# Weight pieces, filler matmuls and store ranks in a planned attention-and-experts kernel

## The chip, the cores and the metric

The kernel runs on one core of a Trainium2 chip. The metric is the device time of one execution in microseconds (us). Six runs of the kernel before gave a median of 307.6 us (307.2 to 310.36). The engines of the core are named as in the profile: PE (TensorE, matmuls; PEld is its weight loading), DVE (VectorE), ACT (ScalarE), POOL (GpSimd) and SP (SyncE, which here only issues transfers).

## What is computed

A gated linear attention with 4 batches, 8 heads, 768 steps and 48 values per head feeds a mixture of 4 experts over 3072 tokens of 384 values, all in float32.

```python
f = 1.0 / (1.0 + np.exp(-f_logit))
for t in range(S):
    state = f[:, :, t, :, None] * state + np.einsum('bhd,bhe->bhde', k[:, :, t], v[:, :, t])
    y[:, :, t] = np.einsum('bhd,bhde->bhe', q[:, :, t], state)
x = y.transpose(0, 2, 1, 3).reshape(B * S, H * D)
p = domain_probs / (domain_probs.sum(-1, keepdims=True) + 1e-09)
for e in range(4):
    out += p[:, e:e + 1] * (np.maximum(x @ w1[e], 0.0) @ w2[e])
```

Here w1[e] is 384 x 1024 and w2[e] is 1024 x 384.

## The kernel before

The 768 steps are cut into six chunks (c = 0 to 5) of 128. For each chunk and batch, attention is done in blocks: the gate (L256, L260), its running sum by a matmul (L264), exponentials (L274, L276), scaled q and k (L288), their transposes (by PE, L297, in chunks 0 and 1, by DMA, L301, later), scores (L312) and their mask (L316), the result y (L323, L327), its transpose into xT (L352 or L305), and the state carried to the next chunk (L333, L340, L347, L348). The last row of the exponentials goes through a small transfer named egs (L283).

A chunk then has 512 tokens (4 batches of 128) for the experts. For each expert e and each block fc of 128 of the 1024 hidden columns, three matmuls over the 384 inputs make h (L356), and ReLU on ACT or DVE (L364, L362) writes it as bf16. For each batch nt, eight matmuls over the hidden blocks, in two halves of four, make the output (L368); it is scaled by p and added to an output tile "o" (L377 or L379 for expert 0, L375 for the others). After expert 3 the tile is stored (L383). In chunk 0, and in chunk 1 for some experts, h is made in two halves of 256 tokens, because the second two batches' attention is done later.

Weights come by POOL's DMA queue in nine pieces (L398 to L409): expert 0's w1 in two halves of columns, then w1 of 1, w2 of 0, w1 of 2, w2 of 1, w1 of 3, w2 of 2, w2 of 3. The first is issued when the last q of chunk 0 has landed. The load of chunk 1's f, batch 1 (L230), waits for the third piece from the end; the last piece waits for k of chunk 1. All other loads, stores, egs and DMA transposes are issued by SP, in one order.

The order of everything is written at build time by a small planner (class Plan, L26 to L99). Each step has a cost on the engines that may do it, a number for its rank (prio, lower goes first), dependencies, and buffers ("rooms") that it takes and frees. Whenever a planned engine is free, the planner gives it the lowest number among the steps that are ready (L73 to L89). DMA is one such engine. A step is ready (L40) when each step before it has ended, plus a latency and that step's lag. The steps are then emitted in the planned order, and the hardware's engines each work through their own list in that order, waiting by semaphores. So a planned time only sets the order.

Rooms: four PSUM banks for h and output sums (ps_m), four for attention (ps_t), six output tiles "o" (four are filled in one chunk), four each for f, q, k, v. Ranks in the expert part go by a running unit (L546 to L552): a step of h has the unit's number, output matmuls that plus 0.5. Chunk 0 has units 0 to 39, its last expert's outputs are units 40 to 47, and chunk 2's loads have 30 to 37 (L577 to L580).

Before the first h, PE's planned gaps are filled with matmuls on a tile of ones (L584 to L595), one for each 0.2 us of gap.

Of the kernel before, what the change touches and what calls it, by code (L numbers as in the profile page):

```python
# [9 lines left out]
BF16 = mybir.dt.bfloat16  # L10
# [15 lines left out]
class Plan:  # L26
# [13 lines left out]
    def ready(self, o, e):  # L40

        t = 0.0
        for d in o.deps:
            if d.end is None:
                return None
            t = max(t, d.end + d.lag + (self.LATENCY if d.engine != e else 0.05))
        return t

    def take(self, o):
# [53 lines left out]
def kernel(  # L103
# [11 lines left out]
    nc = tc.nc  # L115
    B, H, S, D = q.shape
# [7 lines left out]
    E, Din, F = moe_w1.shape  # L124
    KD = Din // 128
    KF = F // 128
    NT = B * T
# [6 lines left out]
    wk = ctx.enter_context(tc.tile_pool(name="wk", bufs=1))  # L134
# [4 lines left out]
    P = Plan(rooms)  # L139


    busy = wk.tile([128, 256], BF16, name="busy")
    nc.vector.memset(busy, 1.0)  # L143
    nc.scalar.preload_act_table_set("natural_log_exp_and_others")
    U = const.tile([T, T], FP32)
# [8 lines left out]
    for nm, nb in (("gp", 2), ("qk", 2)):  # L154
        for i in range(rooms[nm]):
            t = pads[nm, i] = const.tile([T, nb, H, P2], BF16, name=f"{nm}{i}")
# [4 lines left out]
        out=mask01, in_=mask01, compare_op=ALU.is_ge, fill=0.0,  # L161
# [5 lines left out]
    for i in range(2):  # L167
        t = const.tile([MP, B, NP, 2 * D], BF16, name=f"sb{i}")
# [16 lines left out]
    ins = {}  # L185
# [10 lines left out]
    def tl(kind, *key):  # L196

        if (kind, key) not in tiles:
            room = kind if kind in rooms else "ps_m" if kind in ("hp", "op", "pp") else "ps_t"
            slot = P.slot[(room, kind) + key if room.startswith("ps_") else (room,) + key]  # L200
            if room in ("gp", "qk"):
                tiles[kind, key] = pads[room, slot]
            else:
                shape, dt = shapes[kind]
                pool = ps if room.startswith("ps_") else wk
                tiles[kind, key] = pool.tile(shape, dt, name=f"{room}{slot}")
        return tiles[kind, key]

    def after(later, earlier):
        tc.add_manual_dep(later.ins, earlier.ins.name,  # L210
                          mybir.DependencyInfo(mybir.DependencyClass.Sync, mybir.DependencyReason.DATA),
                          reason="order of transfers")
# [17 lines left out]
        if (c, nm, b) == (1, "f", 1):  # L230
            after(ins[c, nm, b], ins["w", w_gate])

    def load_w(i, e, which, cols):
        w, r = (w1_sb, w1_r) if which == 1 else (w2_sb, w2_r)
        ins["w", i] = nc.gpsimd.dma_start(out=w[:, e, :, cols], in_=r[e][:, :, cols])  # L235
        if i == w_gate + 2:
            after(ins["w", i], ins[1, "k", 0])
        if i == 0:
            after(ins["w", 0], ins[0, "q", B - 1])


    def load_p():
# [138 lines left out]
    def store(c, nt, cols):  # L381
        r0 = nt * S + c * T
        nc.sync.dma_start(out=out[r0:r0 + T, cols], in_=tl("o", c, nt)[:, cols])  # L383


    ld = {}
    def add_load(c, nm, b, n, prio, deps=(), cost=None):
        op = P.add(f"ld {nm}{c}.{b}", {"DMA": cost or 1.05 * n}, lambda e: load(c, nm, b, n), prio,
                   deps=deps, takes=[(nm, c, b // 2)], lag=2.0)
        for i in range(n):  # L390
            ld[c, nm, b + i] = op
        return op

    for i, x in enumerate("f0 k0 q0 f1 k1 q1 f2 f3 k2 q2 v0 k3 q3 v1 v2 v3".split()):
        add_load(0, x[0], int(x[1]), 1, -1000 + i)
    add_load(1, "f", 0, 1, -980, cost=0.1)

    pieces = [(0, 1, slice(0, F // 2)), (0, 1, slice(F // 2, F))] + [  # L398
        (e, which, slice(0, F if which == 1 else Din)) for e, which in ((1, 1), (0, 2), (2, 1), (1, 2), (3, 1), (2, 2), (3, 2))]
    wd, w_gate = {}, len(pieces) - 3  # L400
    for i, (e, which, cols) in enumerate(pieces):
        if i == w_gate + 2:
            for x in ((1, "f", 1, 1), (1, "k", 0, 2), (1, "q", 0, 2), (1, "v", 0, 2)):
                add_load(*x, -430 + len(ld), deps=wd[3, 1])
        iss = P.add(f"w issue {i}", {"POOL": 0.8}, lambda _, i=i, x=(e, which, cols): load_w(i, *x),
                    -500 + i, deps=[ld[0, "q", B - 1]] + ([ld[1, "k", 0]] if i > w_gate + 1 else []))
        op = P.add(f"w {i}", {"DMA": 2.25 if i < 2 else 4.5}, lambda _: None,
                   -500 + (0, 0.5, 1, 2, 3, 4, 5, 6, 111)[i], deps=[iss], lag=1.5)
        wd[e, which] = wd.get((e, which), []) + [op]  # L409
    for x in ((1, "f", 2, 2), (1, "k", 2, 2), (1, "q", 2, 2), (1, "v", 2, 2)):  # L410
        add_load(*x, -400 + len(ld), deps=wd[3, 1])
# [2 lines left out]
    xdone, kvdone = {}, {}  # L414
# [94 lines left out]
    hdone, omm, oev = {}, {}, {}  # L509

    def add_h(c, e, fc, n0, n1, xs):
        p, n = unit[0], n1 - n0
        key = ("ps_m", "hp", c, e, fc, n0)
        m = P.add(f"h {c}.{e}.{fc}.{n0}", {"PE": 0.645 * n / NT}, lambda _: mm_h(c, e, fc, n0, n1), p,
                  deps=(wd[e, 1] if (c, e) != (0, 0) else [wd[0, 1][fc * 2 // KF]]) + [t for b in xs for t in xdone[c, b]], takes=[key], lag=0.2, frees=[("xT", c)])
        hdone[c, e, fc, n0] = P.add(f"relu {c}.{e}.{fc}.{n0}",
                                    {"ACT": 0.6, "DVE": 0.69} if n == NT else {"ACT": 0.39, "DVE": 0.42},
                                    lambda g: relu(c, e, fc, n0, n1, g), p - 3, deps=[m],
                                    takes=[("h", c, e)], frees=[key])

    def add_o(c, e, nt, half):
        p = unit[0] + 0.5
        by_cols = (c, e, nt) == (C - 1, E - 1, B - 1)
        part = half if by_cols else 0
        cols = slice(half * Din // 2, (half + 1) * Din // 2) if by_cols else slice(0, Din)
        fcs = range(KF) if by_cols else range(half * 4, half * 4 + 4)
        key = ("ps_m", "op", c, e, nt, part)
        d = [hdone[k] for k in hdone if k[:2] == (c, e) and k[2] in fcs and k[3] <= nt * T]
        m = omm[c, e, nt] = P.add(f"o {c}.{e}.{nt}.{half}", {"PE": 0.645}, lambda _: mm_o(c, e, nt, fcs, part, cols), p,
                                  deps=d + wd[e, 2] + [omm.get((c, e, nt))], takes=[key], lag=0.2, frees=[("h", c, e)])  # L530
        if half == 1 or by_cols:
            w = 0.36 if by_cols else 0.62
            ev = oev[c, e, nt] = P.add(f"ev_o {c}.{e}.{nt}.{part}", {"ACT": 0.58, "DVE": 0.56} if e == 0 else {"DVE": w},
                                       lambda g: ev_o(c, e, nt, part, cols, g), p - 1,
                                       deps=[m, oev.get((c, e - 1, nt)), pdone], takes=[("o", c, nt)], frees=[key])
            if e == E - 1:
                P.add(f"store {c}.{nt}.{part}", {"DMA": 0.6}, lambda _: store(c, nt, cols), p, deps=[ev], frees=[("o", c, nt)])

    attention(0, lambda b, s: -200 + 3.6 * b + s * 0.8, 1)
    pl = P.add("ld p", {"ACT": 0.1}, lambda e: load_p(), -1100, lag=3.0)  # L540
# [2 lines left out]
    ALL, LO, HI = list(range(B)), [0, 1], [2, 3]  # L543
    N2 = NT // 2

    def zip_units(hs, os):  # L546
        for i in range(max(len(hs), len(os))):
            if i < len(hs):
                add_h(*hs[i])
            if i < len(os):  # L550
                add_o(*os[i])
            unit[0] += 1  # L552

    def hl(c, e, n0, n1, xs):
        return [(c, e, fc, n0, n1, xs) for fc in range(KF)]
# [4 lines left out]
    for c in range(C):  # L560
        u0 = unit[0]
        if c == 0:
            for n0, n1, xs in ((0, N2, LO), (N2, NT, HI)):
                zip_units(hl(c, 0, n0, n1, xs), [])
        elif c == 1:
            zip_units([], ol(0, E - 1, ALL))
            for n0, n1, xs in ((0, N2, LO), (N2, NT, HI)):
                zip_units(hl(c, 0, n0, n1, xs), [])
                zip_units(hl(c, 1, n0, n1, xs), ol(c, 0, xs))
        else:  # L570
            zip_units(hl(c, 0, 0, NT, ALL), ol(c - 1, E - 1, ALL))
        for e in range(2 if c == 1 else 1, E):
            zip_units(hl(c, e, 0, NT, ALL), ol(c, e - 1, ALL))
        if c + 1 < C:
            base = u0 + (0 if c else 10)
            attention(c + 1, lambda b, s, base=base: base + 2 + 5 * b + s, 2)
        if c + 2 < C:  # L577
            for half in range(2):
                for j, nm in enumerate("fkqv"):
                    add_load(c + 2, nm, 2 * half, 2, u0 + 30 + 4 * half + j, deps=wd[3, 1])  # L580
# [5 lines left out]
    spare = ps.tile([128, 512], FP32, name="ps_m3")  # L586
    t = 2.5
    for o in done:
        if o.engine == "PE" and o.start <= first:
            o.pad, t = int((o.start - t) / 0.2), o.end  # L590
    if PRINT:
        PRINT(done)
    for o in done:
        for _ in range(o.pad):
            nc.tensor.matmul(out=spare[:, 0:256], lhsT=busy[:, 0:128], rhs=busy, start=True, stop=True)  # L595
        o.emit(o.engine)


# [31 lines left out]
```

## Time and profile before

| what | us |
|---|---|
| median of six runs | 307.6 |
| the profiled execution | 307.2 |
| its span, first to last instruction | 305.4 |
| PE busy | 291.9 |
| ACT, DVE, POOL busy | 171.9, 131.9, 96.4 |
| first h matmul | 23.05 |
| last matmul ends | about 302 |

The profile is of one execution. A page gives totals by engine, 40 slices of the span, and the costliest groups of instructions; the trace behind it answers for waits (who stood idle, and what ended it), for the chain of work that ended last, for a timeline, and for busy time in stretches. In a timeline line the first two numbers are the start and the duration in us, and the bracket is the idle time of that engine before it and what released it; "x4" merges four instructions. A line number is one of the kernel before. PEclk is the clock that was granted to PE. On SP, a line's duration is the time in which the issue held the queue, not the transfer.

### The profile page before, as it was taken

The page shows a single profiled execution, that of the slowest core. Times are in us where ns is not written, and L with a number is a line of the kernel's source. Part 1 is how long each engine was busy: PE and PEld are TensorE (multiplying, and loading weights), DVE is VectorE, ACT ScalarE, POOL GpSimd, SP SyncE. Part 2 cuts the span into 40 slices and gives each one's busy share as a digit, 9 for nine tenths or more (in the row PEclk, how much of TensorE's full clock was granted, in tenths as well). Part 3 has the DMA queues.
Part 4 walks back from the last instruction along what each step waited for, and adds up shares of the span by engine and source line. Part 5 has one row for each costly group of instructions (what it writes and reads, how often), then busy time and mean ns, then how long its engine had stood idle before and what let it go on. Part 6 is the DMA issues. An engine that isn't in the chain of part 4 may idle for free.

```text
span 305.4 us, 5535 instructions
## 1 busy us (share of the span) xinstructions
PE 291.9 (96%) x2121; PEld 171.1 (56%) x2151; DVE 131.9 (43%) x251; ACT 171.9 (56%) x308; POOL 96.4 (32%) x159
## 2 busy tenths in 40 slices
PE   7869999999997999999999999999999999999995
PEld 5648555557774566455555555565555555555553
DVE  5676003588852376506373335363325252201223
ACT  4765763766766464677454676444566444465440
POOL 4384501325676045442624442622232100000000
PEclk9997999999999999999999999999999999999999
DMA  8999999990997539969799988200422300100003
GB/s 150 202 168 207 207 208 200 187 136 2 186 204 164 109 77 179 195 159 169 114 211 165 219 171 150 49 15 13 114 60 50 49 15 24 70 22 2 0 0 105
DMA packets 134639, 36.10 MB, mean 118 GB/s; under 512 B 125372, under 2 KB 133436, under 8 KB 134612
## 3 DMA queue, kind: packets, MB, share of 16 engines
q1 hardware_dynamic: 128416, 29.40, 53.9%
q0 software_dynamic: 6160, 6.29, 12.6%
q8 instruction: 17, 0.28, 0.4%
q14 instruction: 10, 0.08, 0.1%
q10 hardware_dynamic: 36, 0.05, 0.1%
HBM read 31.51 MB, written 4.72 MB: 119 GB/s over the span
## 4 chain that ended last, share of the span: by engine, by line
PE 86%; DMA 7%; SPq 4%; issue 1%; DVE 1%; ACT 0%
PE ps_m L368 40%; PE ps_m L356 39%; SPq L228 3%; DMA w_sb<-in_moe_w_dram 2%; PE ps_t L312 2%; DMA out_dram<-o 2%; DMA q<-in_q_dram 2%; PE ps_t L327 1%; PE ps_t L333 1%; PE ps_t L323 1%; DMA QK<-qk 1%; PE ps_t L264 1%; DVE qk L288 1%; PE ps_t L297 0%; PE ps_t L352 0%
## 5 line engine op out<-in xcount | busy, mean ns | idle before, releaser
L356 PE MATMUL ps_m<-xT,w_sb 128*128 128x512 bf16 (+1 forms) x618 | 150.8, 357 | 5.1 <-ACT o L377 2.0
L364 ACT ACTIVATE h<-ps_m 128x512 bf16<-128x512 f32 (+1 forms) x176 | 98.3, 562 | 97.6 <-PE ps_m L356 90.8
L368 PE MATMUL ps_m<-w_sb,h 128*128 128x384 bf16 x776 | 151.7, 324 | 0.2
L368 PEld LDWEIGHTS <-h 128*128 128x128 bf16 x776 | 73.4, 98 | 56.7
L375 DVE SCALAR_TENSOR_TENSOR o<-ps_m,pn,o 128x384 f32<-128x384 f32 (+1 forms) x73 | 44.6, 611 | 111.0 <-PE ps_m L368 104.2
L356 PEld LDWEIGHTS <-w_sb 128*128 128x128 bf16 x648 | 62.4, 99 | 50.0 <-issue 2.3
L362 DVE TENSOR_SCALAR h<-ps_m 128x512 bf16<-128x512 f32 (+1 forms) x40 | 22.2, 562 | 33.5 <-PE ps_m L356 31.8
L347 POOL TENSOR_TENSOR Sf<-Sf,egs 48x192 f32<-48x192 f32 x40 | 20.4, 511 | 44.2 <-DVE Sf L340 42.2
L316 DVE TENSOR_TENSOR AT<-ps_t,mask 128x512 bf16<-128x512 f32 x48 | 30.2, 683 | 7.6 <-PE ps_t L312 7.5
L288 POOL TENSOR_TENSOR qk<-q,e 128x384 bf16<-128x384 f32 x17 | 20.2, 1187 | 39.0 <-ACT e L274 34.8
L288 POOL TENSOR_TENSOR qk<-k,e 128x384 bf16<-128x384 f32 x22 | 23.4, 1065 | 24.6 <-ACT e L276 17.5
L274 ACT ACTIVATE e<-ps_t 128x384 f32<-128x384 f32 x20 | 17.3, 863 | 4.9 <-PE ps_t L264 2.1
L377 ACT ACTIVATE o<-ps_m,pn 128x384 f32<-128x384 f32 x22 | 12.8, 581 | 8.1 <-PE ps_m L368 5.1
L340 DVE TENSOR_TENSOR Sf<-Sf,ps_t 48x192 f32<-48x192 f32 x40 | 14.0, 350 | 7.1 <-PE ps_t L333 6.3
L348 POOL CAST sb<-Sf 48x192 bf16<-48x192 f32 x40 | 13.6, 340 | 2.6
L235 POOL DMA_DIRECT2D w_sb<-in_moe_w_dram x9 | 7.6, 850 | 19.1 <-DMA k<-in_k_dram 16.7
L224 POOL CAST vb<-v 128x384 bf16<-128x384 f32 x19 | 9.8, 539 | 11.3 <-PE ps_t L333 3.7
L256 ACT ACTIVATE ex<-f 128x768 f32<-128x768 f32 (+1 forms) x14 | 10.5, 748 | 4.5 <-DMA f<-in_f_logit_dram 4.5
L276 ACT ACTIVATE e<-ps_t 128x384 f32<-128x384 f32 x24 | 12.7, 531 | 0.0
L327 PE MATMUL ps_t<-vb,AT 128*128 128x48 bf16 x192 | 11.6, 184 | 0.7 <-ACT vb L222 0.6
L595 PE MATMUL ps_m<-busy 128*128 128x256 bf16 x51 | 10.7, 343 | 1.3 <-DVE busy L143 1.3
L327 PEld LDWEIGHTS <-AT 128*128 128x128 bf16 x192 | 9.9, 97 | 2.8 <-issue 0.8
(53 smaller groups left out, 136.3 us busy)
## 6 DMA issues: line engine op xcount, KB each, us to landing
w_sb<-in_moe_w_dram POOLq DMA_DIRECT2D x7, 768.0 KB, 17.2
out_dram<-o SPq DMA_DIRECT2D x23, 192.0 KB, 2.1
k<-in_k_dram SPq DMA_DIRECT2D x10, 384.0 KB, 5.7
q<-in_q_dram SPq DMA_DIRECT2D x10, 384.0 KB, 6.3
v<-in_v_dram SPq DMA_DIRECT2D x10, 384.0 KB, 5.9
f<-in_f_logit_dram SPq DMA_DIRECT2D x9, 384.0 KB, 5.6
f<-in_f_logit_dram SPq DMA_DIRECT2D x6, 192.0 KB, 4.4
k<-in_k_dram SPq DMA_DIRECT2D x4, 192.0 KB, 4.3
```

Source lines behind the costliest of these rows:

```text
L274: nc.scalar.activation(out=e[:, 0].rearrange("t (d h) -> t h d", d=D), in_=cs[:, 0:HD].rearrange("t (i r d) -> t r i d", r=2, d=D), func=A ...
L288: engines[eng].tensor_tensor(out=tl("qk", c, b)[:, j, :, 0:D].rearrange("t (i r) d -> t i r d", r=2), in0=tl("qk"[j], c, b // 2)[:, hh(b), ...
L316: nc.vector.tensor_tensor(out=tl("AT", c, b)[:, r].rearrange("s i t -> s (i t)"), in0=tl("A", c, b, r).rearrange("s i t -> s (i t)"), in1= ...
L327: nc.tensor.matmul(out=y[:, h * D:(h + 1) * D], lhsT=AT[:, r, i, :], rhs=vb[:, h, :], start=(c == 0), stop=True, skip_group_check=True)
L340: nc.vector.tensor_tensor(out=Sf[rows, b], in0=Sf[rows, b], in1=KV[rows, :, r, :], op=ALU.add)
L347: nc.gpsimd.tensor_tensor(out=Sf[rows, b], in0=Sf[rows, b], in1=eg, op=ALU.mult)
L348: nc.gpsimd.tensor_copy(out=nb[rows, b, :, r * D:(r + 1) * D], in_=Sf[rows, b])
L356: nc.tensor.matmul(out=tl("hp", c, e, fc, n0)[:, n0:n1], lhsT=w1_sb[:, e, kk, fc * 128:(fc + 1) * 128], rhs=tl("xT", c)[:, kk, n0:n1], sta ...
L362: nc.vector.tensor_relu(out=dst, in_=src)
L364: nc.scalar.activation(out=dst, in_=src, func=AF.Relu)
L368: nc.tensor.matmul(out=tl("op", c, e, nt, part)[:, cols], lhsT=tl("h", c, e)[:, fc, nt * T:(nt + 1) * T], rhs=w2_sb[:, e, fc, cols], start ...
L375: nc.vector.scalar_tensor_tensor(out=o, in0=op, scalar=pe, in1=o, op0=ALU.mult, op1=ALU.add)
```

## The change

Five edits, all in the planning:

1. In the planner, a dependency on a step of the same engine no longer adds that step's lag, and on PE adds no latency at all (0.05 us elsewhere).
2. The first three weight matrices come in two pieces each (w1 of expert 0 and 1 by columns, w2 of expert 0 by hidden blocks), eleven in all. A step depends on the half that it reads. The gates on the third piece from the end and on the last one stay.
3. Chunk 0's first expert layer goes by halves of the hidden columns, and within each by halves of tokens. Before, it went by halves of tokens alone.
4. Filler matmuls are 512 columns wide, one for each 0.4 us of planned gap.
5. A store's rank is lowered by 25, so that it goes ahead of more.

```diff
-            t = max(t, d.end + d.lag + (self.LATENCY if d.engine != e else 0.05))
+            t = max(t, d.end + (d.lag + self.LATENCY if d.engine != e else 0.0 if e == "PE" else 0.05))
...
-    busy = wk.tile([128, 256], BF16, name="busy")
+    busy = wk.tile([128, 512], BF16, name="busy")
...
-    def load_w(i, e, which, cols):
+    def load_w(i, e, which, ks, cols):
         w, r = (w1_sb, w1_r) if which == 1 else (w2_sb, w2_r)
-        ins["w", i] = nc.gpsimd.dma_start(out=w[:, e, :, cols], in_=r[e][:, :, cols])
-        if i == w_gate + 2:
-            after(ins["w", i], ins[1, "k", 0])
+        ins["w", i] = nc.gpsimd.dma_start(out=w[:, e, ks, cols], in_=r[e][:, ks, cols])
         if i == 0:
             after(ins["w", 0], ins[0, "q", B - 1])
+        if i == w_last:
+            after(ins["w", i], ins[1, "k", 0])
...
-    pieces = [(0, 1, slice(0, F // 2)), (0, 1, slice(F // 2, F))] + [
-        (e, which, slice(0, F if which == 1 else Din)) for e, which in ((1, 1), (0, 2), (2, 1), (1, 2), (3, 1), (2, 2), (3, 2))]
-    wd, w_gate = {}, len(pieces) - 3
+    every = slice(0, None)
+    pieces = [(e, 1, every, slice(i * F // 2, (i + 1) * F // 2)) for e in range(2) for i in range(2)]
+    pieces += [(0, 2, slice(i * KF // 2, (i + 1) * KF // 2), every) for i in range(2)]
+    pieces += [(e, which, every, every) for e, which in ((2, 1), (1, 2), (3, 1), (2, 2), (3, 2))]
+    w_last, w_gate = len(pieces) - 1, len(pieces) - 3
...
-        op = P.add(f"w {i}", {"DMA": 2.25 if i < 2 else 4.5}, lambda _: None,
-                   -500 + (0, 0.5, 1, 2, 3, 4, 5, 6, 111)[i], deps=[iss], lag=1.5)
+        op = P.add(f"w {i}", {"DMA": 2.25 if i < 6 else 4.5}, lambda _: None, -400 if i == w_last else -460 + i, deps=[iss], lag=1.5)
...
-                  deps=(wd[e, 1] if (c, e) != (0, 0) else [wd[0, 1][fc * 2 // KF]]) + [t for b in xs for t in xdone[c, b]], takes=[key], lag=0.2, frees=[("xT", c)])
+                  deps=[wd[e, 1][fc * len(wd[e, 1]) // KF]] + [t for b in xs for t in xdone[c, b]], takes=[key], lag=0.2, frees=[("xT", c)])
...
-                                  deps=d + wd[e, 2] + [omm.get((c, e, nt))], takes=[key], lag=0.2, frees=[("h", c, e)])
+                                  deps=d + (wd[e, 2] if by_cols or len(wd[e, 2]) == 1 else [wd[e, 2][half]]) + [omm.get((c, e, nt))], takes=[key], lag=0.2, frees=[("h", c, e)])
...
-                P.add(f"store {c}.{nt}.{part}", {"DMA": 0.6}, lambda _: store(c, nt, cols), p, deps=[ev], frees=[("o", c, nt)])
+                P.add(f"store {c}.{nt}.{part}", {"DMA": 0.6}, lambda _: store(c, nt, cols), p - 25, deps=[ev], frees=[("o", c, nt)])
...
-            for n0, n1, xs in ((0, N2, LO), (N2, NT, HI)):
-                zip_units(hl(c, 0, n0, n1, xs), [])
+            for fcs in (range(KF // 2), range(KF // 2, KF)):
+                for n0, n1, xs in ((0, N2, LO), (N2, NT, HI)):
+                    zip_units([x for x in hl(c, 0, n0, n1, xs) if x[2] in fcs], [])
...
-            o.pad, t = int((o.start - t) / 0.2), o.end
+            o.pad, t = int((o.start - t) / 0.4), o.end
...
-            nc.tensor.matmul(out=spare[:, 0:256], lhsT=busy[:, 0:128], rhs=busy, start=True, stop=True)
+            nc.tensor.matmul(out=spare, lhsT=busy[:, 0:128], rhs=busy, start=True, stop=True)
```

More of the change, by code (lines that the diff above doesn't have):

```diff
@@ L396 @@
     add_load(1, "f", 0, 1, -980, cost=0.1)
-    pieces = [(0, 1, slice(0, F // 2)), (0, 1, slice(F // 2, F))] + [
-        (e, which, slice(0, F if which == 1 else Din)) for e, which in ((1, 1), (0, 2), (2, 1), (1, 2), (3, 1), (2, 2), (3, 2))]
-    wd, w_gate = {}, len(pieces) - 3
-    for i, (e, which, cols) in enumerate(pieces):
-        if i == w_gate + 2:
+    every = slice(0, None)
[3 more added lines that the diff above has]
+    w_last, w_gate = len(pieces) - 1, len(pieces) - 3
+    wd = {}
+    for i, (e, which, ks, cols) in enumerate(pieces):
+        if i == w_last:
             for x in ((1, "f", 1, 1), (1, "k", 0, 2), (1, "q", 0, 2), (1, "v", 0, 2)):
                 add_load(*x, -430 + len(ld), deps=wd[3, 1])
-        iss = P.add(f"w issue {i}", {"POOL": 0.8}, lambda _, i=i, x=(e, which, cols): load_w(i, *x),
-                    -500 + i, deps=[ld[0, "q", B - 1]] + ([ld[1, "k", 0]] if i > w_gate + 1 else []))
-        op = P.add(f"w {i}", {"DMA": 2.25 if i < 2 else 4.5}, lambda _: None,
-                   -500 + (0, 0.5, 1, 2, 3, 4, 5, 6, 111)[i], deps=[iss], lag=1.5)
+        iss = P.add(f"w issue {i}", {"POOL": 0.8}, lambda _, i=i, x=(e, which, ks, cols): load_w(i, *x),
+                    -500 + i, deps=[ld[0, "q", B - 1]] + ([ld[1, "k", 0]] if i == w_last else []))
+        op = P.add(f"w {i}", {"DMA": 2.25 if i < 6 else 4.5}, lambda _: None, -400 if i == w_last else -460 + i, deps=[iss], lag=1.5)
         wd[e, which] = wd.get((e, which), []) + [op]
```

## The prediction, made before the changed kernel was run

> **What bounds the kernel now.** I read the engine totals first, then the slices, then the waits of TensorE, then the timeline around each gap, and the queue of SP last. TensorE is the bound:
>
> ```profile
> PE 291.9 (96%) x2121; PEld 171.1 (56%) x2151; DVE 131.9 (43%) x251; ACT 171.9 (56%) x308; POOL 96.4 (32%) x159
> PEclk9997999999999999999999999999999999999999
> ```
>
> PE is idle 305.4 - 291.9 = 13.5 us, and the clock dips once. The table by stage places the idle time: 5.60 us before the first expert matmul at 23.05 (23.05 - 17.45), 0.25 from 23.05 to 60, 0.70 from 60 to 65, 2.05 from 90 to 97, 3.43 after the last matmul (from 301.96), and 1.45 in pieces of 0.05 over the 205 us between. TensorE's own waits name the two that matter:
>
> ```profile
> PE ps_m L356 <- ACT o L377: 2.0, 1, 2.0
> PE ps_m L356 <- DMA w_sb<-in_moe_w_dram: 1.8, 1, 1.8
> ```
>
> The second is the wait for the first weight piece, which ends at 23.05. The first is one stall of 2.00 us that ends at 95.81, and the timeline shows what lies behind it:
>
> ```profile
> 89.52 2.55 SPq L383 DMA_DIRECT2D out_dram<-o  x2
> 95.18 1.13 ACT L377 ACTIVATE o<-ps_m,pn 128x384 f32<-128x384 f32 x2 [2.25 <-DMA out_dram<-o]
> 95.81 4.05 PE L356 MATMUL ps_m<-xT,w_sb 128*128 128x256 bf16 x20 [2.00 <-ACT o L377]
> ```
>
> ScalarE wants a third output tile for chunk 1 (six "o" buffers, four held by chunk 0) and must wait until chunk 0's first store has landed. That store is issued at 89.52 and lands 5.63 us later (the chain's "89.52 5.63 DMA out_dram<-o"). But its data had long been ready: VectorE's last four adds of chunk 0 (L375, expert 3) start at 67.83, 70.09, about 70.7 and 72.69 and take 0.62 each, so the four tiles are ready at 68.45, 70.7, 71.4 and 73.3. The store was held by its place on SP, behind eight loads of chunk 2:
>
> ```profile
> 75.37 0.61 SPq L228 DMA_DIRECT2D f<-in_f_logit_dram  x1
> ...
> 87.89 1.54 SPq L228 DMA_DIRECT2D v<-in_v_dram  x1
> 89.52 2.55 SPq L383 DMA_DIRECT2D out_dram<-o  x2
> ```
>
> **Ranked stores.** The planner gives a DMA to the lowest number that is ready. Chunk 0's stores are numbered by their unit: 41.5 to 47.5 before, 16.5 to 22.5 after. Chunk 2's loads are 30 to 37 (u0 = 0, plus 30 to 37). So today every such load that is ready goes first; after, each ready store does. SP issues in the planned order; chunk 1's egs transfers (numbers 15 to 30) lie in the same stretch, the last two issued at 74.19 and 74.74 because they wait for ScalarE. All four tiles are ready by 73.3, so I expect all stores on SP by about 75 and landed by 81 (5.63 after issue at worst). The third tile is wanted at 92.93 (95.18 - 2.25). The cover is 12 us and the wait goes: **-2.00 us** on TensorE, which is the path here. What is late next? Chunk 2's first score matmuls (L312) run at 104.98, 103 after the change. Their operands come by transposes on SP at 94.89 and 98.20; the four stores that sit between 89.52 and 96.83 take 2.55 + 0.54 + 0.52 = 3.6 us of SP away from there, so they come earlier too. What the move pushes back: egs of chunk 1's batches 1 to 3, each behind at most the store that waits until 73.3. The one at 71.80 would go at about 74 and land 1.7 us later (its landing today); VectorE and POOL want it from 81.09. Then the eight loads, if a store were issued after 75.33: 0.54 us of SP each. Nothing by my order.
>
> **Weight pieces in halves.** Issues on POOL (L235) go from 9 to 11. Two more at 0.83 us (6.68 us for 8) make POOL busy to 24.9 in place of 23.3; it is idle until 27.40, so nothing waits. The bytes are the same. By the landings of L235 the pieces arrive at 23.0, 25.5 (halves), 29.6, 33.5, 37.2, 41.0, 44.7, 48.7: two halves cost 2.5 us for the second, against 3.7 to 4.1 for a whole piece, so a half may cost 0.4 to 0.6 us more than half a whole. Four halves for two wholes: the pieces behind come 0 to 2 us later. The first output matmul (L368) needs expert 0's second matrix, here at 33.5, and starts at 35.41 behind busy TensorE, and by the new dependency its first half is enough, which lands about 2 us before the whole; the cover holds. Chunk 1's loads of f (1,1) and on are gated by the piece landing at 44.7; their consumers run from 54.27 (ScalarE, f landed about 50) and 67.36 (f of batch 2, landed at 61.6): cover 4 to 6 us. Cost 0, bounds 0 to +0.7 (the wait at 60 to 62 doubles).
>
> The Trainium skill, "DMA: Bandwidth & Descriptors", section "Bandwidth", speaks against halving: batch transfers to at least 1 MiB; its section on the SWDGE path fits 2.0 us of fixed time per DMA. As an estimate, were that fixed time serial, two more DMAs would move expert 0's second matrix from 33.5 to 37.5, past the 36.1 at which its second half is wanted, and the change would be worth some 1.4 us less. The trace has the halves at 203 to 226 GB/s in the slices from 21 to 27 and wholes at 192 to 218 from 30 to 47, so it does not show that cost as serial; no part of my sum uses it.
>
> **First layer by column halves.** Matmul count and shapes stay (48 of 128x256). Today the order is all eight column blocks for tokens 0 to 255, then the others; the fifth block needs the second piece, which lands at 25.5, and the weight loads wait 0.44 us for it at 25.55. After, four blocks of the other tokens may come between; their xT (L224 and L222 at 24.88 to 25.26) is there 0.2 us before the piece. Of 0.44 some is covered by the matmul in flight: I take **-0.2 us** (bounds -0.44 to +0.2, should that xT be later).
>
> **Cold clock and fillers.** From 23.80 to 27.00 the granted clock is 0.50 while TensorE is busy all 3.20 us: 1.6 us lost, after the idle 21.3 to 23.05. Between the last attention matmul at 20.75 and 23.05 the plan puts no filler today (a planned gap under 0.2 us). A filler now needs 0.4. The wait for the first piece is DMA and stays, so the gap and the dip stay: 0. Fillers elsewhere: 51 of 256 columns become at most 25 of 512; groups of 14 and 8 become 7 and 4, and single ones vanish. By halving and rounding down each group of the timeline (14, 8, 1, 6, 1, 1, 2, 2, 1, 3, 3, 1, 3, 1, 4) I get 21, or 42/51 of the columns. The memset of their operand (0.27 us, L143) doubles at most: the first filler starts 0.3 later, and nothing waits for it. If thinner filling lets the clock fall before 23.05, the matmuls from 23.05 to 23.80 run at half speed, +0.4 us; if a filler lands ahead of the first expert matmul and keeps the clock, -1.6.
>
> The Trainium skill, "TensorE: Matmul & The Clock Gate", section "What's actually happening", has the clock fall after at least one idle window of about 3.4 us. By it a gap of 1.75 us would cost nothing and the dip would be no part of any gain or loss. The trace shows the dip after 1.75 us of idleness; I go by the trace.
>
> **The planner's latencies.** The 0.05 between dependent steps on one engine, and the lag with it, are dropped on PE; elsewhere the lag. So the second half of an output group may follow its first at once, and chunk 1's loads are planned 1.5 us earlier. SP's real gate for these loads is the landing at 44.7, so chunk 1's attention is placed up to 1.5 us earlier against loads that have 4 us. The stall pair before the transposes L297 (0.43 at 60.34, 0.31 at 61.91, VectorE's products of 1.6 us) may go or grow: 0, bounds -0.7 to +0.7. In the tail the last add is of 192 columns (302.01) today and stays so; its 3.43 us of add, store and landing stay: 0 (bounds -0.3 to +0.3).
>
> **Sum.** -2.00 - 0.2 = -2.2. The profiled execution took 307.2 (span 305.4, 1.8 around it), and so 305.0. The median of the runs is 307.6, 0.4 above; I predict the median: 307.6 - 2.2 = **305.4 us**. Its own range, from the bounds without the clock: -0.44 - 0.7 - 0.3 against +0.2 + 0.2 + 0.7 + 0.7 + 0.3 worst; two of them together, 304.3 to 306.4.
>
> **Rivals.** *Clock or wait gained too* (0.14): the dip goes (-1.6), alone or with the 0.7 at 60: 303.1 to 303.8. For it: the plan of the head shifts; against: the wait for the first piece is untouched. *The stores don't help* (0.12): the planned order still puts them behind the loads, or the 2.00 us return as another wait on the same six buffers: 307.4. For it: in the plan, the loads may start while SP in truth still waits for egs; against: their readiness at 68 to 73. *Slower* (0.14): SP works in order, and the stores stand between egs and the load of chunk 2's f, which is issued at 75.37 and used by ScalarE at 79.86, already tight (issue to landing is 3.3 us at the least, 5.5 median). Four stores cost 4 x 0.54 = 2.2 us, or 2 x 2.55 = 5.1 as at 89.52 under load; 5.1 less a slack of 0 to 1 leaves ScalarE waiting 4 to 5 us with ReLUs behind it. A wait of 2.25 there cost TensorE 2.00 at 95.81, so 4.0 to 4.4: 307.6 - 2.2 + 4.2 = 309.6. It decides once more than about 2.5 us of stores stand after 75.33.
>
> **How the numbers follow.** Forecast 0.60, the three rivals 0.14, 0.12, 0.14. 0.5% (1.5 us) is about what a measurement of this kernel can tell from no change: 306.1 and 309.1 are the bounds. Faster: 0.14 and 0.56 of the forecast's 0.60: 0.70. Same: 0.12, the forecast's rest of 0.04 and 0.01 of the slower: 0.17. Slower: 0.13. The range takes in the forecast, most of the clock gain and the stores' failure: 303.4 to 308.0.
>
> **What would show it.** Right: four stores on SP before 76, no wait of ScalarE L377 on out_dram, PE busy throughout 90 to 97, some 20 fillers of 512 columns, a dip still at about 24. Wrong: SP's loads of chunk 2 starting after 77, ScalarE's L256 waiting near 80, a new idle gap on PE of over 1 us anywhere between 27 and 301.

## The result and the profile after

The changed kernel takes 304.78 us (median of 31 runs, 303.71 to 305.80). The kernel before, on the same chips, takes 307.14 (median of 68 runs, 304.59 to 311.07). The ratio is 0.9934 (95% interval 0.9919 to 0.9949), so 2.0 us less (1.6 to 2.5). It compares means and leaves out two executions of the kernel before that ran in a slower state; the medians differ by 2.4. The profiled execution took 304.48 with a span of 302.8, 2.6 under that of before.

On the page after, the engine totals and the clock:

```profile
PE 289.2 (96%) x2088; PEld 167.2 (55%) x2120; DVE 133.5 (44%) x254; ACT 170.5 (56%) x305; POOL 97.8 (32%) x161
PEclk9998999999999999999999999999999999999999
```

TensorE is as full as before, of a shorter span, and the dip in the fourth slice is still there. TensorE's waits after (total, times, longest):

```profile
PE ps_t L327 <- ACT vb L222: 2.0, 2, 1.5
PE ps_t L297 <- DVE qk L288: 1.7, 5, 0.6
PE ps_m L356 <- DMA w_sb<-in_moe_w_dram: 0.9, 1, 0.9
```

No line names ScalarE's L377 any more. The wait for the first weight piece fell from 1.8 to 0.9, but a new one of 1.5 (L327 for the cast of v) stands ahead of it at 20.18, and the first expert matmul comes only 0.14 earlier, at 22.91. Of the new fillers there are 18. Where the stall was, the table by stretch has TensorE busy for 4.95 of 7 us before (first fence) and 6.95 after (second; the first figure of a line is the length, the next TensorE's busy time):

```profile
90.00:97.00 7.00, 4.95 (x37) 3.46 (x36) 1.94 (x5) 3.46 (x8) 3.22 (x5) 1.00 0.95 182
```

```profile
90.00:97.00 7.00, 6.95 (x47) 4.46 (x47) 2.97 (x7) 5.69 (x10) 4.38 (x7) 1.00 1.13 158
```

SP's timeline after shows why. The four stores stand among chunk 1's egs, and the loads of chunk 2 come behind:

```profile
67.68 2.31 SPq L383 DMA_DIRECT2D out_dram<-o  x2
70.08 1.24 SPq L283 DMA_DIRECT2D egs<-e  x2
71.41 2.65 SPq L383 DMA_DIRECT2D out_dram<-o  x2
74.15 2.41 SPq L283 DMA_DIRECT2D egs<-e  x4
76.61 0.58 SPq L228 DMA_DIRECT2D f<-in_f_logit_dram  x1
```

The stores are out by 74.06 (71.41 + 2.65), 15 us earlier than the first was before. ScalarE's third tile of chunk 1 waits for its matmul alone:

```profile
92.95 0.58 ACT L377 ACTIVATE o<-ps_m,pn 128x384 f32<-128x384 f32 x1 [0.61 <-PE ps_m L368]
```

To see where the 2.6 us of the profiles come from, the same expert matmul can be followed through two traces: when is the n-th weight load of L356 (h) issued? In both kernels the work behind a number is nearly the same, so a step in the difference is time won or lost there.

| n-th h weight load | before, us | after minus before | what lies in the step |
|---|---|---|---|
| 0 | 23.05 | -0.14 | the first piece lands a little earlier |
| 72 | 41.09 | -0.29 | the dip and the second piece: -0.15 |
| 144 | 75.65 | +0.09 | chunk 1's attention: +0.38 |
| 216 | 96.35 | -2.07 | the stall: -2.16 |
| 288 | 128.70 | -2.08 | nothing |
| 384 | 174.88 | -2.55 | chunk 3's attention: -0.47 |
| last | 295.50 | -2.55 | nothing |

From 175 us on, the two traces run side by side to the last matmul.

### The profile page after: what moved, and what is told of

Its sections match the earlier page's. It is cut to its first block, busy times and chain, and to the rows that moved or that the text cites. A ratio compares the mean times of both kernels' runs of the same rounds, so it can differ in the third digit from the quotient of the medians.

```text
span 302.8 us, 5467 instructions
## 1 busy us (share of the span) xinstructions
PE 289.2 (96%) x2088; PEld 167.2 (55%) x2120; DVE 133.5 (44%) x254; ACT 170.5 (56%) x305; POOL 97.8 (32%) x161
## 4 chain that ended last, share of the span: by engine, by line
PE 89%; DMA 4%; SPq 3%; issue 1%; DVE 1%; ACT 0%
PE ps_m L368 41%; PE ps_m L356 40%; SPq L228 3%; DMA w_sb<-in_moe_w_dram 2%; PE ps_t L312 2%; DMA q<-in_q_dram 2%; PE ps_t L327 1%; DVE qk L288 1%; PE ps_t L323 1%; PE ps_t L333 1%; PE ps_t L264 1%; PE ps_t L297 1%; PE ps_t L352 0%; ACT e L274 0%; DVE o L375 0%
## 5 line engine op out<-in xcount | busy, mean ns | idle before, releaser
L364 ACT ACTIVATE h<-ps_m 128x512 bf16<-128x512 f32 (+1 forms) x173 | 96.9, 563 | 100.8 <-PE ps_m L356 93.0
L356 PE MATMUL ps_m<-xT,w_sb 128*128 128x512 bf16 (+1 forms) x618 | 150.9, 357 | 2.3 <-DMA w_sb<-in_moe_w_dram 0.9
L368 PE MATMUL ps_m<-w_sb,h 128*128 128x384 bf16 (+1 forms) x776 | 151.5, 324 | 0.2
L356 PEld LDWEIGHTS <-w_sb 128*128 128x128 bf16 x648 | 62.4, 99 | 46.6 <-DMA w_sb<-in_moe_w_dram 1.0
L288 POOL TENSOR_TENSOR qk<-q,e 128x384 bf16<-128x384 f32 x19 | 22.4, 1184 | 47.7 <-ACT e L274 41.7
L362 DVE TENSOR_SCALAR h<-ps_m 128x512 bf16<-128x512 f32 (+1 forms) x43 | 23.7, 564 | 27.1 <-PE ps_m L356 24.2
L288 POOL TENSOR_TENSOR qk<-k,e 128x384 bf16<-128x384 f32 x20 | 20.9, 1043 | 16.4 <-ACT e L276 11.0
L235 POOL DMA_DIRECT2D w_sb<-in_moe_w_dram x11 | 9.0, 824 | 19.4 <-DMA k<-in_k_dram 15.7
L377 ACT ACTIVATE o<-ps_m,pn 128x384 f32<-128x384 f32 x22 | 12.8, 581 | 3.1 <-PE ps_m L368 2.3
L327 PE MATMUL ps_t<-vb,AT 128*128 128x48 bf16 x192 | 11.4, 184 | 2.0 <-ACT vb L222 2.0
L327 PEld LDWEIGHTS <-AT 128*128 128x128 bf16 x192 | 10.0, 97 | 4.0 <-issue 2.1
L260 ACT ACTIVATE gp<-ex 128x768 bf16<-128x768 f32 (+1 forms) x14 | 10.5, 749 | 0.3
```

The costliest lines, as they stand in the source:

```text
L288: engines[eng].tensor_tensor(out=tl("qk", c, b)[:, j, :, 0:D].rearrange("t (i r) d -> t i r d", r=2), in0=tl("qk"[j], c, b // 2)[:, hh(b), ...
L327: nc.tensor.matmul(out=y[:, h * D:(h + 1) * D], lhsT=AT[:, r, i, :], rhs=vb[:, h, :], start=(c == 0), stop=True, skip_group_check=True)
L356: nc.tensor.matmul(out=tl("hp", c, e, fc, n0)[:, n0:n1], lhsT=w1_sb[:, e, kk, fc * 128:(fc + 1) * 128], rhs=tl("xT", c)[:, kk, n0:n1], sta ...
L362: nc.vector.tensor_relu(out=dst, in_=src)
L364: nc.scalar.activation(out=dst, in_=src, func=AF.Relu)
L368: nc.tensor.matmul(out=tl("op", c, e, nt, part)[:, cols], lhsT=tl("h", c, e)[:, fc, nt * T:(nt + 1) * T], rhs=w2_sb[:, e, fc, cols], start ...
```

## The experiments

Each kernel was timed against the kernel before on the same chip; three groups of four ran on three chips. Changes are to the kernel before or after, as said. In the words on record, "theory" is at first that of the prediction.

### The rank of the stores alone

```diff
-                P.add(f"store {c}.{nt}.{part}", {"DMA": 0.6}, lambda _: store(c, nt, cols), p, deps=[ev], frees=[("o", c, nt)])
+                P.add(f"store {c}.{nt}.{part}", {"DMA": 0.6}, lambda _: store(c, nt, cols), p - 25, deps=[ev], frees=[("o", c, nt)])
```

> The kernel before with the store's rank lowered by 25 and nothing else. My theory (the late store is the whole gain but 0.2 us): chunk 0's four stores are issued by 76 us, the 2.00 us wait of TensorE at 94 to 96 is gone, and the time is 2.0 us (0.65%) under the kernel before. Rival 1 (the gain comes from the head: halves, order of columns, fillers): the wait may go, but the time falls by under 0.7 us. Rival 2 (the wait returns elsewhere): TensorE idle over 1 us in a new place between 60 and 300, time as before.

Measured: 303.31 us (6 runs, 302.79 to 304.40), ratio 0.9889 (0.9860 to 0.9918): 3.4 us less, more than all five edits together give. The table by stretch, with TensorE busy throughout:

```profile
90.00:97.00 7.00, 7.00 (x44) 4.16 (x43) 3.06 (x7) 5.55 (x10) 4.05 (x6) 1.00 0.82 107
```

Its stores are out early:

```profile
66.78 2.62 SPq L383 DMA_DIRECT2D out_dram<-o  x2
70.74 1.25 SPq L383 DMA_DIRECT2D out_dram<-o  x2
```

Rival 1 falls: no other edit is needed. The late store's place is the cause. The size was expected at 2.0, below the interval (2.5 to 4.3). In the profiles 4.3 us lie between the two: 2.16 at the stall and 0.47 in chunk 3, which together are in the interval, and 1.70 by the 24th weight load. That last part is no work of this edit: TensorE's order is the same up to 80 us. It is how two executions differ, the first expert matmul at 21.89 in place of 23.05 and no dip.

### The changed kernel without the rank

The same line, the other way, in the changed kernel.

> The changed kernel with the old rank of its stores. My theory: the stores again stand behind chunk 2's loads on SP, TensorE stands still about 2 us near 94, and the time is 0 to 0.4 us under the kernel before, 2.0 above the changed one. Rival 1 (the gain comes from the head and the planner's latencies): 1.5 to 2.4 us under the kernel before.

Measured: 306.36 us (12 runs, 305.32 to 308.36), ratio 0.9983 (0.9958 to 1.0008). The gain is gone, as the theory said. This kernel's wait of TensorE, SP's queue, the store from issue to landing (in the chain that ended last), and ScalarE's wait for it:

```profile
PE ps_m L356 <- ACT o L377: 1.1, 1, 1.1
```

```profile
90.71 2.62 SPq L383 DMA_DIRECT2D out_dram<-o  x2
```

```profile
90.71 4.75 DMA out_dram<-o
```

```profile
95.48 1.13 ACT L377 ACTIVATE o<-ps_m,pn 128x384 f32<-128x384 f32 x2 [1.61 <-DMA out_dram<-o]
```

The stall is back with its cause, at 1.1 us in place of the 2 expected. TensorE's work there and the store's issue are both 1.2 us later than in the profile of before, but the store landed 4.75 us after its issue, not 5.63. So the buffer came free only 0.3 later, and the wait is 0.9 shorter: between these two profiles its length goes with the time that the store took to land.

### Eight output tiles, stores as late as before

```diff
-             "vb": 7, "egs": 8, "QK": 4, "AT": 2, "yb": 2, "xT": 2, "h": 2, "o": 6}
+             "vb": 7, "egs": 8, "QK": 4, "AT": 2, "yb": 2, "xT": 2, "h": 2, "o": 8}
```

> The kernel before with eight output tiles in place of six, and nothing else: the stores stay late, but nobody needs their buffers. My theory (the buffer is what TensorE waited for): no wait near 94, and 2.0 us under the kernel before. Rival (the place of the stores on SP costs by itself, by holding back egs and the transposes of chunk 2): little or no gain, under 0.7 us, or a wait of TensorE at its score matmuls near 103.

Measured: 303.72 us (6 runs, 302.94 to 304.05), ratio 0.9893 (0.9866 to 0.9921). SP's queue and the table by stretch:

```profile
88.66 2.54 SPq L383 DMA_DIRECT2D out_dram<-o  x2
```

```profile
90.00:97.00 7.00, 7.00 (x46) 4.30 (x44) 2.56 (x5) 4.82 (x11) 3.80 (x5) 1.00 0.87 191
```

The store is issued as late as ever, and TensorE does not stop. So the wait was for the buffer, and the stores' place on SP costs next to nothing by itself: the two ways of ending the wait give the same gain within their intervals. The rival falls.

### The old fillers in the changed kernel

```diff
-    busy = wk.tile([128, 512], BF16, name="busy")
+    busy = wk.tile([128, 256], BF16, name="busy")
...
-            o.pad, t = int((o.start - t) / 0.4), o.end
+            o.pad, t = int((o.start - t) / 0.2), o.end
...
-            nc.tensor.matmul(out=spare, lhsT=busy[:, 0:128], rhs=busy, start=True, stop=True)
+            nc.tensor.matmul(out=spare[:, 0:256], lhsT=busy[:, 0:128], rhs=busy, start=True, stop=True)
```

> The changed kernel with its fillers as before: 256 columns, one for each 0.2 us of planned gap. My theory: the clock dip near 24 stays, the time is that of the changed kernel within 0.4 us. Rival (thinner filling lets the clock fall earlier): TensorE's clock falls later than 22.2 by about 1.5 us, and the time is 0.4 to 1 us under the changed kernel.

Measured: 304.39 us (8 runs, 303.49 to 306.85), ratio 0.9924 (0.9889 to 0.9959): by the time, undecided. The profile has no dip at all, against my theory, and a wait that had not been seen, in TensorE's list:

```profile
PE ps_m L356 <- DVE psm L252: 1.2, 1, 1.2
```

At 25.34 an expert matmul waits for VectorE's normalisation of the probabilities, which holds one of the four PSUM banks. With TensorE at full speed the column order has taken away the wait for the second weight piece and run into this one.

So the rank alone beats the change, and the question was which of the other four edits gives 1 to 1.5 us away. The next four kernels start from the rank and add to it.

### Rank and the planner's latencies

```diff
-            t = max(t, d.end + d.lag + (self.LATENCY if d.engine != e else 0.05))
+            t = max(t, d.end + (d.lag + self.LATENCY if d.engine != e else 0.0 if e == "PE" else 0.05))
```

> The kernel before with the store rank and the planner's new latencies. The rank alone gave 303.3 us, all five edits 304.8: some of the other four cost 1.5 us together. Theory A (the new fillers: the clock dips in every execution): this one stays at 303.3, within 0.5. Theory B (the latencies: chunk 1's attention is placed earlier and TensorE waits 0.4 us more between 55 and 75): 303.7, with that wait in the profile. Theory C (pieces and column order): 303.3.

Measured: 304.29 us (11 runs, 303.54 to 306.85), ratio 0.9920 (0.9884 to 0.9955). In its profile TensorE has a new wait at chunk 1's second transposes:

```profile
72.14 0.40 PE L297 MATMUL ps_t<-ident,qk 128*128 128x128 bf16 x4 [0.20 <-DVE qk L288]
```

By weight loads the kernel loses 0.37 us against the rank alone up to n = 144, as the changed kernel does at the same place, and 0.42 more between 119 and 137 us, which the changed kernel does not. Theory B holds in kind, in place (the wait at 72 lies in the 55 to 75 expected) and in the size of its first part.

### Rank, halved pieces and column order

The first layer's loop, the pieces and their dependencies as in the change; fillers and latencies as before.

> The kernel before with the store rank, the halved pieces and the column order. Theory A: 303.3 within 0.5. Theory B: 303.3 within 0.5. Theory C (the column order removes a wait of 1.0 to 1.4 us for the second weight piece where the clock does not dip, but TensorE then waits 1.2 us for the PSUM bank that the probabilities hold): no gain, 303.3 to 304.3, with a wait on L252 or L253 of 1 us near 24. Rival to C: the wait for the second piece goes and nothing comes back: 302.3.

Measured: 303.11 us (6 runs, 302.79 to 303.23), ratio 0.9845 (0.9799 to 0.9892). Its list of TensorE's waits has the same line:

```profile
PE ps_m L356 <- DVE psm L252: 1.2, 1, 1.2
```

Theory C holds as to its mechanism: the order's gain returns as another wait of the same size, and the time is that of the rank alone. It loses nothing that the times show, so it is not what was sought.

### Rank and the new fillers

The three lines of the old fillers' diff, the other way, in the kernel with the rank alone.

> The kernel before with the store rank and the new fillers (512 columns, one for each 0.4 us). Theory A: the clock dips in all or nearly all executions, and the first expert matmul comes no earlier: 304.0 to 305.0. Theories B and C: 303.3 within 0.5.

Measured: 304.56 us (6 runs, 302.76 to 305.83), ratio 0.9891 (0.9842 to 0.9939). Its table by stretch, and that of the rank alone (the third figure from the end is the granted clock, 0.50 or 1.00 in the second lines):

```profile
20.00:23.00 3.00, 1.40 (x24) 0.80 (x23) 0.78 (x2) 2.02 (x5) 3.00 (x4) 0.98 1.17 175
23.00:26.00 3.00, 2.79 (x15) 2.11 (x16) 0.72 (x2) 0.97 (x3) 0.07 (x1) 0.50 1.15 211
```

```profile
20.00:23.00 3.00, 2.16 (x27) 1.56 (x25) 1.21 (x4) 1.85 (x5) 2.85 (x4) 1.00 1.22 206
23.00:26.00 3.00, 1.99 (x28) 1.61 (x26) 2.50 (x9) 1.16 (x4) 0.30 (x1) 1.00 1.16 212
```

With the dip TensorE is busy 2.79 of 3 us and does 15 matmuls; without it, 1.99 and 28. The dip costs less than it seems, because at full speed 1.0 us goes on waiting for the second piece. Net of that, the profile with new fillers loses 0.69 us from the first expert matmul to n = 72, and starts that matmul 1.3 us later, which I do not lay at the fillers' door. Theory A holds in direction; the runs spread over 3 us, and the interval does not part this kernel from the rank alone. Each execution's mean granted clock says more (the table below): five of the six had a lowered clock, 303.76 to 305.83 us, and the one that had not took 302.76, as fast as any of the rank alone.

### Probabilities ranked first

```diff
-    pp = P.add("pp", {"PE": 0.6}, lambda e: pe_pp(), -1, deps=[pl], takes=[("ps_m", "pp")], lag=0.2)
-    pdone = P.add("probs", {"DVE": 0.9}, lambda e: probs(), 4, deps=[pp] + xdone[0, B - 1], frees=[("ps_m", "pp")])
+    pp = P.add("pp", {"PE": 0.6}, lambda e: pe_pp(), -900, deps=[pl], takes=[("ps_m", "pp")], lag=0.2)
+    pdone = P.add("probs", {"DVE": 0.9}, lambda e: probs(), -900, deps=[pp], frees=[("ps_m", "pp")])
```

> As the kernel with rank, halved pieces and column order, but the four VectorE steps of the probabilities are ranked first and wait only for their transposes, so that their PSUM bank is free before the first expert matmul. Theory C: the wait of 1.2 us near 24 is gone in executions without a dip, and the time is 0.5 to 1.2 us under that kernel, about 302.5. Rival (TensorE would wait for xT or a weight piece there instead): within 0.4 us of it.

Measured: 303.32 us (6 runs, 303.04 to 304.58), ratio 0.9861 (0.9817 to 0.9905): the rival's case. The wait on L252 is gone, and TensorE's list has two on weights in its place:

```profile
PE ps_m L356 <- DMA w_sb<-in_moe_w_dram: 1.1, 2, 0.7
```

These waits are only part of it. By weight loads the kernel is 0.39 us ahead of that with pieces alone at n = 72, and loses 0.37 in chunk 1, to the stall that the latencies gave, here without them:

```profile
71.80 0.40 PE L297 MATMUL ps_t<-ident,qk 128*128 128x128 bf16 x4 [0.20 <-DVE qk L288]
```

### Fillers over the wait for the first piece

In the kernel with rank, pieces and column order:

```diff
-            o.pad, t = int((o.start - t) / 0.2), o.end
+            o.pad, t = int((o.start - t) / 0.2) + (8 if o.start == first else 0), o.end
```

> The kernel with rank, halved pieces and column order (303.1 us), with eight more fillers of 256 columns (0.87 us) just ahead of the first expert matmul, where TensorE waits for the first weight piece. If the wait there is what lets the clock dip: no dip after 20 in the profile, and a time of 303.1 or up to 0.3 less, with a spread under 1 us. Rival (the dip is set by the thin stretch from 10 to 20, or the fillers delay the first matmul): 303.1 to 304.0.

Measured: 303.04 us (6 runs, 302.79 to 305.51), ratio 0.9858 (0.9802 to 0.9915). No dip in the profile, but one run of 305.51. It changes nothing that can be told.

### No fillers after 9 us

In the kernel with the rank alone:

```diff
-            o.pad, t = int((o.start - t) / 0.2), o.end
+            o.pad, t = int((o.start - t) / 0.2) if o.start < 9.0 else 0, o.end
```

> The kernel before with the store rank (303.3 us), without the fillers after the first 22 (none after 9 us). Theory A (thin filling lets the clock dip, and a dip costs the expert stage 0.5 to 1 us): a dip after 12 in every execution, first expert matmul 0 to 1 us later, 304.0 to 305.0. Rival (fillers after 9 us do nothing for the time): 303.3 within 0.4.

Measured: 304.63 us (6 runs, 303.76 to 305.10), ratio 0.9892 (0.9839 to 0.9945). The table by stretch:

```profile
16.00:20.00 4.00, 3.08 (x38) 2.36 (x39) 3.65 (x8) 2.69 (x5) 3.55 (x5) 0.50 1.30 186
20.00:23.00 3.00, 1.96 (x25) 1.44 (x25) 1.09 (x3) 2.02 (x5) 3.00 (x4) 0.50 1.23 193
23.00:26.00 3.00, 3.00 (x17) 2.27 (x16) 1.05 (x3) 0.97 (x3) 0.11 (x1) 0.50 1.15 214
```

The clock is at half from 11.4 to 28.4, and yet the first expert matmul comes at 22.56, 0.67 after that of the rank alone; the attention of chunk 0 has the slack. What is lost is 1.64 us from there to n = 24. All six executions had a mean clock of 0.966 to 0.977. This is the strongest form of theory A, and its 304.63 lies where the changed kernel's times lie.

### The changed kernel without the latencies, and the changed kernel again

The first of the two has the latencies' line as before.

> The changed kernel without the planner's new latencies. If they cost 0.4 to 0.8 us (as the rank with latencies showed, 304.3 against 303.3): 304.0 to 304.4 against 304.8 for the changed kernel, and no wait of 0.4 us between 55 and 60 in the profile. Rival (the latencies cost nothing beside the fillers): 304.8.

> The changed kernel itself, on the chip of the three beside it: 304.8 us, a dip near 22 to 24 in the profile.

Measured: 303.93 us (6 runs, 302.95 to 304.18), ratio 0.9868 (0.9810 to 0.9925), and 304.46 (6 runs, 303.74 to 304.70), ratio 0.9886 (0.9834 to 0.9938). Half a microsecond, in ranges that overlap. The profiles agree: first the kernel without the latencies, then the changed kernel:

```profile
65.00:75.00 10.00, 10.00 (x108) 7.46 (x105) 8.44 (x18) 6.58 (x14) 3.88 (x5) 1.00 0.34 94
```

```profile
65.00:75.00 10.00, 9.80 (x103) 7.11 (x102) 7.95 (x17) 6.71 (x14) 3.00 (x3) 1.00 0.35 94
```

By weight loads, the changed kernel loses 0.36 to 0.38 us here in both of its profiles, and this one nothing. The wait was expected between 55 and 60; it stands at 73.22. The dip of the changed kernel's second profile begins at 21.64.

## Why the prediction was right, point by point

**The sum.** 305.4 was forecast, 304.8 measured, in the range; -2.2 against -2.0 (-1.6 to -2.5). Most of the 0.6 between the two times is the base: 307.6 in six runs, 307.14 in 68.

**The stall.** -2.00 was forecast, 2.16 is the step in the traces. Buffer, late store and place on SP were the right chain: taking the lateness away, or the need for the buffer, gives the same. The stores went out by 74.1, against "by about 75". The rival in which the stores do not help falls with this. The loads behind them were put at nothing; they started at 76.61, 1.2 later than before, though TensorE's work was at most 0.4 later. The stores push egs back, as forecast, and egs the loads: in the rank alone these are 0.8 earlier than before where TensorE's work is 1.7 earlier. ScalarE had no trouble with it. The rival that ends slower needed about 2.5 us of stores after 75.33: there were none.

**Weight pieces.** The cost was forecast at 0 and bounded by pieces landing up to 2 us later. They land at 22.9, 24.8, 26.7, 28.6, 30.5 and 32.5, then 36.2, 40.1 and 43.8: a half costs 1.9 to 2.0 us, a whole 3.7 to 3.9, and the piece that gates chunk 1's loads came 0.9 us earlier. Here the trace decides against the fixed 2.0 us for each DMA in the Trainium skill, "DMA: Bandwidth & Descriptors", section "Anatomy of one DMA — SWDGE (gpsimd) path", if one reads it as serial: two halves cost at most 0.3 us more than a whole.

**Column order.** -0.2 was forecast. The wait for the second piece did go, but where the clock is full a wait of 1.2 us for the probabilities' PSUM bank takes its place, and where it dips nothing was to be won. In the times it is worth nothing that could be told. The step's fault was to size the wait in a profile with a dip. The weight loads waited 0.44 us there (first line), which I took for 0.2 of TensorE, and 1.29 at full speed in the rank alone (second), where TensorE itself waited 1.01:

```profile
25.55 0.34 PEld L356 LDWEIGHTS <-w_sb 128*128 128x128 bf16 x3 [0.44 <-DMA w_sb<-in_moe_w_dram]
24.55 0.22 PEld L356 LDWEIGHTS <-w_sb 128*128 128x128 bf16 x3 [1.29 <-DMA w_sb<-in_moe_w_dram]
```

**Fillers and clock.** This step was wrong in kind. I took the dip as a fixture of the program, caused by the wait for the first piece, and the new fillers' cost as 0. The dip is a matter of the execution, and of the filling. Of the profiles with the old fillers (before, rank, eight tiles, old fillers, rank and latencies, rank and pieces, probabilities, filled wait) one of eight has a dip that touches the expert stage; of those with the new ones (changed kernel twice, no rank, rank and fillers, without latencies) all five, beginning at 20.3 to 23.8. Profiles are few, but the mean granted clock of every execution is on record. One dip of 3.41 us at half takes 0.006 off it, so 0.997 or more is called full here:

| kernel | executions at full clock | their median, us | median of the others, us |
|---|---|---|---|
| before | 15 of 46 | 306.01 | 308.02 |
| rank alone | 5 of 6 | 303.27 | 304.40 |
| eight tiles | 6 of 6 | 303.72 | none |
| rank and latencies | 6 of 11 | 303.94 | 306.12 |
| rank and pieces | 4 of 6 | 303.12 | 303.08 |
| rank and new fillers | 1 of 6 | 302.76 | 304.80 |
| old fillers in the changed kernel | 3 of 8 | 303.59 | 305.48 |
| changed kernel | 0 of 31 | none | 304.78 |

Over all kernels but that without late fillers, 47 of 95 executions with the old fillers ran at full clock, and 2 of 61 with the new ones. So the old fillers do not rule a dip out, and with the new ones there nearly always is one. The mean does not say where a dip lies; one at 14.8 in the profile of rank and pieces cost nothing that shows.

The price was put at +0.4 for a fall before 23.05, and the dip of the profile before was read as 1.6 lost; the runs show 0.5 to 0.7 net in profiles, up to 1.6 with no late fillers. In the times, the kernel before takes 2.0 more without a full clock, so something goes with the dip, perhaps the late first expert matmul. That the wait for the first piece has a part in it is not excluded: with a dip in the expert stage the first expert matmul starts at 22.55 to 23.90 in seven profiles, without one at 21.89 to 22.49 in six, and at 22.89 only where eight more fillers stand ahead of it.

**Latencies.** 0 was forecast, bounds -0.7 to +0.7; the traces show +0.36 to +0.38 in chunk 1, in the times 0.5 with overlapping ranges. I had chosen the middle because two old stalls might go; they stayed (0.44 at 60.05, 0.31 at 61.63) and a third came. All five profiles with the new latencies lose 0.36 to 0.38 there, and of the nine others only that with the probabilities first, so it is the planned order that costs, to which the latencies are one way.

**What was not forecast.** 0.47 us in chunk 3's attention. Before, the weight loads of the scores wait 0.5 us for the transposes of chunk 3's q and k (PEld L312 on DMA QK), and after they do not. The rank alone gains the 0.47 as well, but so does the changed kernel without the rank, within 0.08, while eight tiles fall 0.30 short of it. So it goes with the planned order that each edit happens to give, not with one edit, and it was not taken apart.

So the one large term was right, and the rest came out by luck. In the two traces, which both have a dip, -2.16 at the stall, -0.47 in chunk 3, -0.29 in the head and +0.38 in chunk 1 make 2.5 us less. The times give 2.0, which fits a clock that falls in every execution of the changed kernel and in two of three of the kernel before. Three effects that the sum had at nothing (chunk 3, latencies, fillers) about cancel. The change holds a better one: the rank alone, or with pieces and column order, takes 303.0 to 303.3 us in four kernels, 1.1 to 1.7 under the changed one (304.5 and 304.8). The ranges of rank with pieces (302.79 to 303.23) and of the changed kernel (303.71 to 305.80) do not touch, though they come from different chips. On one chip, the rank with pieces and eight more fillers took 303.04 and the changed kernel 304.46.

**What stays open.** The kernel before spreads over 305 to 311 us, the rank alone over 302.8 to 304.4, and the rank's 3.4 us are more than the 2.6 of the two steps named above. The granted clock accounts for much of both. At full clock the kernel before takes 305.0 to 306.9 us, and the rank is 2.8 under it on the same chip (303.27 against 306.10), close to the 2.6. The rest goes with the clock, which was lowered in 12 of 19 executions of the kernel before there, and in one of the rank's six. Why so is not shown. It may be chance, or the stall may lower the clock itself where its 2 us of idle TensorE fall into one window of the clock; in the one profile of the kernel before, the edge of a window at 95.32 (21 windows of 3.41 us after the dip's start at 23.64) cuts the stall, and the clock stays. Nor is it settled why the first expert matmul starts between 21.9 and 23.9 with the same loads ahead of it.

## What to carry to other kernels

When an engine waits for a buffer, look past the wait to when the data that holds the buffer was ready: 16 us lay here between the last add and the store's issue, and a rank or two more tiles end it equally well. Try each part of a bundle alone, since one edit that wins can hide others that lose. And do not price a wait from a stretch where the clock is low: the weight loads' wait of 0.44 us seen there was 1.29 at full speed. Set the granted clock beside each time as well: six executions can differ from six others by how many had a dip.

## What the runs showed of the hardware that was not expected

POOL had at most eight of these transfers under way. In the changed kernel's timeline the ninth and tenth issue wait for the first and second piece to land (at 22.9 and 24.8):

```profile
23.16 0.74 POOL L235 DMA_DIRECT2D w_sb<-in_moe_w_dram  x1 [0.26 <-DMA w_sb<-in_moe_w_dram]
25.07 0.92 POOL L235 DMA_DIRECT2D w_sb<-in_moe_w_dram  x1 [1.18 <-DMA w_sb<-in_moe_w_dram]
```

Whether the limit is the queue's or the program's is not shown. It kept POOL until 26.0, not 24.9 as forecast, and POOL's next work came at 27.66.

The granted clock changes in steps of 3.41 us: the dips lasted 3.41 us, or 17.07 = 5 x 3.41 with no late fillers, and they begin at another time in each profile. The Trainium skill, "TensorE: Matmul & The Clock Gate", section "What's actually happening", has a free-running window of 3413 ns, which agrees. It has the fall after a window of idleness; here the changed kernel's dip at 22.19 followed 3.41 us in which TensorE was busy for 1.50, so the measurement says that less than idleness is enough:

```profile
18.78:22.19 3.41, 1.50 (x24) 0.90 (x23) 1.21 (x2) 2.07 (x5) 3.41 (x6) 1.00 1.28 203
```

Cut into such windows at the clock's own changes, the first 100 us of the 14 profiles (from where the clock is recorded) have seven at full clock in which TensorE was busy for 0.54 to 1.82 us, and all seven were followed by half clock. With more than that the clock mostly stayed: it did after 1.90 (the window with most of the stall, in the kernel before), and fell after 2.25 and 2.36. So a busy share of some 55% held the clock in most windows, not in all.
